# Attention and a two-layer MLP in one kernel: half of ten MLP blocks begun among the first heads, with fewer load buffers and w_in loaded by row halves

## The chip, the cores and the metric

The kernel runs on one core of one Trainium2 chip. The metric is the device time of one execution in microseconds (us). The kernel before took 426.06 us (median of 5 runs, 422.62 to 428.41).

## What is computed

`q`, `k` and `v` are fp32 arrays of 8 batches x 12 heads x 448 positions x 64. `w_in` is 768 x 2048 and `w_out` is 2048 x 768, both fp32. The output is 3584 x 768 fp32.

```python
scores = (1 / sqrt(64)) * q @ k.T                 # per batch and head, 448 x 448
attn = softmax(scores)
attn_out = attn @ v                               # 8, 12, 448, 64
x = attn_out.transpose(0, 2, 1, 3).reshape(8 * 448, 768)
h = x @ w_in
g = maximum(0.01 * h, h)
out = g @ w_out
```

## The kernel before

**Units.** Two heads make a unit `u`; there are 6 units a batch (`HP`) and 48 in all. A unit goes through these steps, each a function of the kernel:

- `load(u)` (L90): three DMAs of 224 KB, q, k and v in fp32, issued by SP in the order of the code (only the k of unit 0 is issued by ACT). The tiles come from a pool with 5 buffers for each of the three names.
- `cast(u)` (L103): POOL turns q, k and v into bf16 (L108, L109, L110). The q and k halves go into one tile of a pool of 4, v into one of 5 fixed tiles.
- `transposes(u)` (L163): eight PE transposes into PSUM (L169) and one DVE copy (L172) into `qkT`, for units 0 to 11; later units are turned by a DMA transpose that SP issues (L157).
- `scores(u, c)` (L176): two PE matmuls (L181) for each of 4 chunks of keys; `expo(u, c)` (L188): one ACT exponential (L190) over both heads.
- `pv(u, j)` (L192): sixteen PE matmuls (L199) for head `j`; a column of ones in v gives the softmax sums. DVE takes the reciprocals (L206) and multiplies (L207) into an x tile.
- `x_transposes(u)` (L211): four PE transposes (L220) and a DVE copy (L221) into `xT`, where the rows of the MLP's contraction are: unit `hp` of a batch is contraction slice `kk = hp`. From unit 9 on a DMA transpose does it.

**PSUM.** `scores` has 3 double-bank tiles of its own. Everything else on PE, the transposes, `pv`, and both products of the MLP, shares the two tiles with the tag "g" (`ps_g`), so that PE can write the third of these only when the first has been emptied.

**MLP.** The 3584 tokens are cut into 8 tiles of 384 and 512 tokens in turn (`cuts`); tile 0 has 384. `mlp(i)` (L242) makes for each of 16 blocks `m` six matmuls over `kk` (L250) and one Prelu on ACT from PSUM (L254), then for each 128 tokens and each half of the output 16 matmuls (L268), a DVE copy (L272) and the stores.

**Order.** Tile's scheduling is off, so each engine executes in the order in which the code issues. First the 6 units of batch 0 go through `first(u)` (L278), then the last two `pv` and transposes (L335 to L340). From there the MLP is a generator that yields after each block, and `cluster(g)` (L303), which holds 3 chunks of scores with the `pv`, casts, loads and transposes that belong to them, is called between yields when the matmul columns used have passed the next equal share (L352). Tile 0 has clusters 8 to 18, the first of them ahead of its first block. The third exponential of a cluster is put off to the next `settle()`, which follows the Prelu of a block.

**Weights.** `load_w()` (L119) issues the next weight DMA on POOL's software queue, in POOL's own order among the casts. It reads fp32 and writes bf16, 768 KB each. `w_in` comes in four steps of 512 columns with all 6 slices `kk`, `w_out` in four of 8 row blocks x 384 columns. One is issued ahead of `first(0)`; the others in `first(2)` (1), `first(3)` (2), `first(4)` (2) and `first(5)` (2), always ahead of that unit's cast.

Of the kernel before, what the change touches and what calls it, by code (L numbers as in the profile page):

```python
# [9 lines left out]
F32 = mybir.dt.float32  # L10
# [6 lines left out]
def kernel(  # L17
# [26 lines left out]

    const_pool = ctx.enter_context(tc.tile_pool(name="const", bufs=1))
    w_pool = ctx.enter_context(tc.tile_pool(name="weights", bufs=1))
    ld_pool = ctx.enter_context(tc.tile_pool(name="ld", bufs=5))
    cast_pool = ctx.enter_context(tc.tile_pool(name="cast", bufs=4))
    v_pool = ctx.enter_context(tc.tile_pool(name="vones", bufs=1))
    qk_pool = ctx.enter_context(tc.tile_pool(name="qk", bufs=1))  # L50
    exp_pool = ctx.enter_context(tc.tile_pool(name="exp", bufs=1))
    r_pool = ctx.enter_context(tc.tile_pool(name="rec", bufs=4))
    x_pool = ctx.enter_context(tc.tile_pool(name="x", bufs=3))
    xT_pool = ctx.enter_context(tc.tile_pool(name="xT", bufs=1))
    h_pool = ctx.enter_context(tc.tile_pool(name="h", bufs=2))
    o_pool = ctx.enter_context(tc.tile_pool(name="o", bufs=3))

# [53 lines left out]

    w_steps = []
    for i in range(4):
        w_steps.append((w_in_sb[:, :, ts(i, DF // 4)], w_in_v[:, :, ts(i, DF // 4)]))
    for i in range(4):
        at = (slice(None), ts(i % 2, MD // 2), ts(i // 2, NW))
        w_steps.append((w_out_sb[at], w_out_v[at]))
# [1 line left out]
    def load_w(n=1):  # L119
        for _ in range(n):  # L120
            if w_steps:
                o, i = w_steps.pop(0)
                nc.gpsimd.dma_start(out=o, in_=i)

    load(0, (nc.sync, nc.scalar, nc.sync))
    for i in range(1, 5):
        load(i)

    warm = const_pool.tile([P, 512], BF16)
# [15 lines left out]
        nc.gpsimd.memset(t[:, QL:], 0.0)  # L145
    cast(0, (nc.vector.tensor_copy, nc.scalar.copy, nc.gpsimd.tensor_copy))
    load_w()
    cast(1)
    cast(2)


    x_t = {}
# [35 lines left out]
    def expo(u, c):  # L188
        e = e_sb[u % NE][:, :EL].rearrange("p (j c s) -> p j c s", j=2, c=NSC)
        nc.scalar.activation(e[:, :, c, :], sc_t.pop((u, c))[:SC, :, :S], AX.Exp, scale=scale)  # L190
# [47 lines left out]
    def settle():  # L238
        while late:
            expo(*late.pop(0))  # L240

    def mlp(i):  # L242

        n = cuts[i + 1] - cuts[i]
        at = cuts[i] % NX
        h = h_pool.tile([P, MD, 4 * P], BF16, name="h")
        for m in range(MD):
            ps = ps_g.tile([P, 4 * P], F32, name="mm", tag="g")
            for kk in range(KD):
                nc.tensor.matmul(  # L250
                    ps[:, :n], w_in_sb[:, kk, ts(m, P)], xT[:, kk, at:at + n],
                    start=(kk == 0), stop=(kk == KD - 1),
                )
            nc.scalar.activation(h[:, m, :n], ps[:, :n], AX.Prelu, alpha=0.01)  # L254
            settle()
            yield KD * n

        todo = [(c, w) for c in range(n // P) for w in range(2)]
        if i == 0:
            todo.sort(key=lambda cw: cw[1])  # L260
        o = {}
        for c, w in todo:
            settle()
            if c not in o:
                o[c] = o_pool.tile([P, DM], F32, name="o")
            ps = ps_g.tile([P, 4 * P], F32, name="mm", tag="g")
            for m in range(MD):
                nc.tensor.matmul(  # L268
                    ps[:, :NW], h[:, m, ts(c, P)], w_out_sb[:, m, ts(w, NW)],
                    start=(m == 0), stop=(m == MD - 1),  # L270
                )
            nc.vector.tensor_copy(o[c][:, ts(w, NW)], ps[:, :NW])  # L272
            if w == 1:
                store(o.pop(c), cuts[i] + c * P)
            yield MD * NW


    def first(u):  # L278

        scores(u, 0)  # L280
        scores(u, 1)
        expo(u, 0)
        if u == 0:
            warm_up(4)
        expo(u, 1)
        if u >= 2:
            x_transposes(u - 2)
        if u >= 1:
            pv(u - 1, 0)
        load(u + 5)  # L290
        load_w({2: 1, 3: 2, 4: 2, 5: 2}.get(u, 0))
        if u + 1 < HP:
            transposes(u + 1)
        scores(u, 2)
        scores(u, 3)
        expo(u, 2)
        expo(u, 3)
        cast(u + 3)
        if u >= 1:
            pv(u - 1, 1)  # L300


    def cluster(g):  # L303
# [13 lines left out]
        for a, c in chunks[:2]:  # L317
            expo(a, c)
        late.extend(chunks[2:])
        for a, j in heads:  # L320
            pv(a, j)
            if j == 1 and a >= NPE - 3:
                x_transposes(a)
# [8 lines left out]
    warm_up(2)  # L332
    for u in range(HP):
        first(u)
    u = HP - 1  # L335
    pv(u, 0)
    x_transposes(u - 1)
    pv(u, 1)
    transposes(HP)
    x_transposes(u)  # L340


    begin = [8 * (i + 1) + 3 for i in range(B)]
    begin[0] = 8
    for i in range(B):
        work = list(range(begin[i], begin[i + 1])) if i + 1 < B else []
        n = cuts[i + 1] - cuts[i]
        total = MD * KD * n + n // P * MD * DM
        used, done = 0, 0
        lead = 1 if i == 0 else 0  # L350

        def catch_up():  # L352
            nonlocal done
            while done < len(work) and used * (len(work) - lead) >= total * (done + 1 - lead):
                settle()
                cluster(work[done])
                done += 1

        catch_up()
        for step in mlp(i):  # L360
            used += step
            catch_up()
# [30 lines left out]
```

The softmax here doesn't subtract the row's maximum and nothing guards it: scores larger than these inputs give would overflow.

## Time and profile before

The profiled execution took 426.06 us, of which 424.3 us are the span in which engines work; it is also the median one. The span by stage, from the trace (busy us of each engine in the stage; PE clock as a share of full speed):

| stage, us from the start | what runs | PE | DVE | ACT | POOL | PE clock | DMA, GB/s |
|---|---|---|---|---|---|---|---|
| 5 to 20 | units 0 to 3 | 12.05 | 6.13 | 11.92 | 8.20 | 1.00 | 250 |
| 20 to 36 | units 3 to 5, cluster 8 | 14.00 | 7.55 | 9.87 | 13.38 | 0.74 | 247 |
| 36 to 64 | MLP tile 0, first product, with clusters | 26.59 | 7.22 | 20.25 | 9.22 | 0.96 | 248 |
| 64 to 88 | MLP tile 0, second product, with clusters | 23.55 | 7.79 | 11.35 | 6.31 | 1.00 | 225 |
| 88 to 400 | tiles 1 to 7 | 310.99 | 65.90 | 173.37 | 52.91 | 1.00 | 132 |

Busy time of PE counts matmuls that run at half clock or that overlap in its pipeline, so a busy PE is not a full one. Where a view lists who waited, "PE tr L169 <- POOL qkb L109" means that PE's transposes at line 169 stood still until POOL's cast at line 109 had finished. "DMA fk<-in_k_dram" is a load of k, "SPq" and "POOLq" are the queues of DMA instructions on SP and POOL, q1 is the hardware queue of SP and q0 the software queue of POOL, which carries the weights only.

### The profile page before, as it was taken

What the parts mean: (1) busy time and instruction counts of PE and PEld (TensorE: products, weight loads), DVE (VectorE), ACT (ScalarE), POOL (GpSimd) and SP (SyncE); (2) the same over time, 40 slices, a digit from 0 to 9 for tenths busy, and PEclk for the clock granted to TensorE, in tenths of its full rate; (3) what the DMA queues carried; (4) which work ended last, traced back from release to release, by engine and by line L of the source; (5) the groups of instructions that cost most, each with busy time, mean ns of one, the idle gap of its engine ahead of it and who ended that gap; (6) DMA issues with size and microseconds to landing.
All of it is one profiled execution on the core that took longest, in us unless ns stands there. A gap on an engine that the chain in (4) does not pass through costs nothing.

```text
span 424.3 us, 8986 instructions
## 1 busy us (share of the span) xinstructions
PE 409.9 (97%) x3717; PEld 236.1 (56%) x3731; DVE 99.8 (24%) x271; ACT 228.3 (54%) x322; POOL 91.2 (21%) x168
## 2 busy tenths in 40 slices
PE   7789999999999999999999999999999999999995
PEld 2555556554565656554465656654465666654562
DVE  1552322320122312221132212321032311320021
ACT  4875773667724584467644476456742577214200
POOL 4494330431311212131130213122120200000000
PEclk9987999999999999999999999999999999999999
DMA  8999999996485946777365785779275420230022
GB/s 207 252 246 246 249 250 217 221 243 136 97 168 151 211 111 170 193 157 181 87 158 142 199 153 124 194 142 225 65 172 149 119 56 13 60 86 2 0 76 74
DMA packets 98505, 63.66 MB, mean 150 GB/s; under 512 B 55456, under 2 KB 94880, under 8 KB 98464
## 3 DMA queue, kind: packets, MB, share of 16 engines
q1 hardware_dynamic: 90928, 56.56, 56.3%
q0 software_dynamic: 7296, 6.29, 9.2%
q8 instruction: 29, 0.48, 0.5%
q10 hardware_dynamic: 240, 0.23, 0.2%
q14 instruction: 12, 0.10, 0.1%
HBM read 45.61 MB, written 11.01 MB: 133 GB/s over the span
## 4 chain that ended last, share of the span: by engine, by line
PE 90%; DMA 5%; DVE 2%; SPq 1%; issue 1%; ACT 1%; POOL 0%; ACTq 0%
PE mm L250 34%; PE mm L268 33%; PE pv L199 12%; PE sc L181 9%; DMA fk<-in_k_dram 2%; DMA fq<-in_q_dram 1%; DMA fv<-in_v_dram 1%; PE tr L169 1%; DVE x L207 1%; SPq L157 1%; DVE o L272 1%; ACT e L190 0%; SPq L97 0%; DVE rec L206 0%; PE tr L220 0%
## 5 line engine op out<-in xcount | busy, mean ns | idle before, releaser
L190 ACT ACTIVATE e<-sc 112x896 bf16<-112x896 f32 x192 | 164.4, 917 | 105.9 <-PE sc L181 105.7
L250 PE MATMUL mm<-xT,w_in_sb 128*128 128x384 bf16 (+1 forms) x754 | 150.6, 354 | 1.4 <-DVE x L207 0.7
L268 PE MATMUL mm<-w_out_sb,h 128*128 128x384 bf16 x896 | 150.5, 326 | 0.6 <-DVE x L207 0.3
L268 PEld LDWEIGHTS <-h 128*128 128x128 bf16 x896 | 85.8, 98 | 55.4 <-DVE x L207 0.5
L250 PEld LDWEIGHTS <-w_in_sb 128*128 128x128 bf16 x768 | 73.4, 98 | 67.1 <-issue 1.4
L254 ACT ACTIVATE h<-mm 128x384 bf16<-128x384 f32 (+1 forms) x128 | 69.6, 544 | 61.4 <-PE mm L250 60.3
L110 POOL CAST v<-fv 112x512 bf16<-112x512 f32 x48 | 29.6, 616 | 212.5 <-PE pv L199 184.3
L199 PEld LDWEIGHTS <-e 112*128 112x128 bf16 x1536 | 57.6, 99 | 29.8 <-issue 18.5
L199 PE MATMUL pv<-v,e 112*128 112x65 bf16 x1536 | 66.9, 195 | 2.8 <-ACT e L190 1.4
L272 DVE COPY o<-mm 128x384 f32<-128x384 f32 x56 | 31.2, 557 | 133.7 <-PE mm L268 133.7
L206 DVE RECIPROCAL rec<-pv 112x4 f32<-112x4 f32 x96 | 17.5, 182 | 158.8 <-PE pv L199 158.8
L181 PE MATMUL sc<-qkT 64*128 64x448 bf16 x384 | 49.8, 358 | 0.8 <-DVE qkT L172 0.4
L207 DVE TENSOR_TENSOR x<-pv,rec 112x256 bf16<-112x256 f32 x96 | 40.7, 424 | 3.3
L108 POOL CAST qkb<-fq 112x512 bf16<-112x512 f32 x47 | 28.9, 615 | 22.9 <-DMA qkT<-qkb 11.7
L109 POOL CAST qkb<-fk 112x512 bf16<-112x512 f32 x47 | 28.9, 614 | 10.4 <-DMA fk<-in_k_dram 10.3
L181 PEld LDWEIGHTS <-qkT 64*128 64x128 bf16 x384 | 13.8, 94 | 19.9 <-issue 10.7
L169 PE MATMUL tr<-ident,qkb 112*128 112x112 bf16 x96 | 8.3, 234 | 2.3 <-POOL qkb L109 1.7
L172 DVE COPY qkT<-tr 128x896 bf16<-128x896 bf16 x12 | 7.4, 620 | 12.7 <-PE tr L169 12.5
L169 PEld LDWEIGHTS <-qkb 112*128 112x128 bf16 x96 | 6.1, 109 | 4.6 <-POOL qkb L109 2.2
L135 PE MATMUL mm<-warm 128*128 128x512 bf16 x15 | 5.2, 486 | 1.2 <-DVE warm L130 1.2
L221 DVE COPY xT<-tr 128x448 bf16<-128x448 bf16 x9 | 3.5, 389 | 7.5 <-PE tr L220 7.5
L220 PE MATMUL tr<-ident,x 112*128 112x112 bf16 x36 | 3.7, 231 | 0.2
(17 smaller groups left out, 15.1 us busy)
## 6 DMA issues: line engine op xcount, KB each, us to landing
fq<-in_q_dram SPq DMA_DIRECT2D x48, 224.0 KB, 3.7
fv<-in_v_dram SPq DMA_DIRECT2D x48, 224.0 KB, 4.5
fk<-in_k_dram SPq DMA_DIRECT2D x47, 224.0 KB, 4.0
w_in_sb<-in_moe_w_in_dram POOLq DMA_DIRECT2D x4, 768.0 KB, 15.6
w_out_sb<-in_moe_w_out_dram POOLq DMA_DIRECT2D x4, 768.0 KB, 35.3
out_dram<-o SPq DMA_DIRECT2D x8, 336.0 KB, 3.0
out_dram<-o SPq DMA_DIRECT2D x8, 288.0 KB, 2.7
out_dram<-o SPq DMA_DIRECT2D x8, 240.0 KB, 3.2
```

Of the source, the lines that this page charges most:

```text
L108: by[0](qk_sb[u][:, 0].rearrange("p so h d -> p h so d"), fq)
L109: by[1](qk_sb[u][:, 1].rearrange("p so h d -> p h so d"), fk)
L110: by[2](v_sb[u % NV][:, :, :, :D], fv)
L169: nc.tensor.transpose(tr[:, i, ts(so, SC)], qk_sb[u][:, i, so], ident[:SC, :SC])
L181: nc.tensor.matmul(ps[:, j, :S], t[j * D:(j + 1) * D, S + c * SC:S + c * SC + P], t[j * D:(j + 1) * D, :S], start=True, stop=True,)
L190: nc.scalar.activation(e[:, :, c, :], sc_t.pop((u, c))[:SC, :, :S], AX.Exp, scale=scale)
L199: nc.tensor.matmul(ps[:, qc, :], e[:, at:at + P], vt[:, j, c, :], start=(c == 0), stop=(c == NSC - 1),)
L207: nc.vector.tensor_mul(x_t[u][:, :, j, :], ps[:SC, :, :D], rec.to_broadcast([SC, NSC, D]))
L250: nc.tensor.matmul(ps[:, :n], w_in_sb[:, kk, ts(m, P)], xT[:, kk, at:at + n], start=(kk == 0), stop=(kk == KD - 1),)
L254: nc.scalar.activation(h[:, m, :n], ps[:, :n], AX.Prelu, alpha=0.01)
L268: nc.tensor.matmul(ps[:, :NW], h[:, m, ts(c, P)], w_out_sb[:, m, ts(w, NW)], start=(m == 0), stop=(m == MD - 1),)
L272: nc.vector.tensor_copy(o[c][:, ts(w, NW)], ps[:, :NW])
```

## The change

- The load pool goes from 5 to 3 buffers, the pool of cast q and k from 4 to 2. Three units are loaded ahead instead of five; units 3 and 4 are loaded between the first casts, and in `first(u)` the load of unit `u + 5` comes after the cast of unit `u + 3` instead of ahead of the transposes. `cast(2)` moves into `first(0)`.
- `w_in` is loaded by halves of the contraction (3 slices `kk`) and halves of the columns (1024), upper half first, still four DMAs of 768 KB. Two of them are issued ahead of `first(0)`, one each in `first(2)` and `first(3)`; `w_out` in `first(4)` and `first(5)` as before.
- `fill(1)` makes one block's sum over `kk` = 0, 1, 2 (three matmuls of 384 columns) in a "g" tile, and DVE copies it in fp32 to SBUF (`part`). Ten are made: three in `first(4)`, three in `first(5)`, two after it and two in cluster 8.
- In tile 0's first product these ten blocks then have three matmuls (`kk` = 3, 4, 5), a DVE add of the PSUM sum to `part`, and the Prelu reads `part` in SBUF. The other six blocks are whole and stand between them.
- `transposes(6)` moves into `first(5)`; `x_transposes(5)` moves into cluster 8, which is called ahead of the MLP; clusters 9 to 18 are spread over tile 0's remaining columns.

```diff
--- before.py
+++ after.py
@@ -44,14 +44,15 @@
 
     const_pool = ctx.enter_context(tc.tile_pool(name="const", bufs=1))
     w_pool = ctx.enter_context(tc.tile_pool(name="weights", bufs=1))
-    ld_pool = ctx.enter_context(tc.tile_pool(name="ld", bufs=5))
-    cast_pool = ctx.enter_context(tc.tile_pool(name="cast", bufs=4))
+    ld_pool = ctx.enter_context(tc.tile_pool(name="ld", bufs=3))
+    cast_pool = ctx.enter_context(tc.tile_pool(name="cast", bufs=2))
     v_pool = ctx.enter_context(tc.tile_pool(name="vones", bufs=1))
     qk_pool = ctx.enter_context(tc.tile_pool(name="qk", bufs=1))
     exp_pool = ctx.enter_context(tc.tile_pool(name="exp", bufs=1))
     r_pool = ctx.enter_context(tc.tile_pool(name="rec", bufs=4))
     x_pool = ctx.enter_context(tc.tile_pool(name="x", bufs=3))
     xT_pool = ctx.enter_context(tc.tile_pool(name="xT", bufs=1))
+    part_pool = ctx.enter_context(tc.tile_pool(name="part", bufs=1))
     h_pool = ctx.enter_context(tc.tile_pool(name="h", bufs=2))
     o_pool = ctx.enter_context(tc.tile_pool(name="o", bufs=3))
 
@@ -111,7 +112,8 @@
 
     w_steps = []
     for i in range(4):
-        w_steps.append((w_in_sb[:, :, ts(i, DF // 4)], w_in_v[:, :, ts(i, DF // 4)]))
+        at = (slice(None), ts(i // 2, KD // 2), ts(i % 2, DF // 2))
+        w_steps.append((w_in_sb[at], w_in_v[at]))
     for i in range(4):
         at = (slice(None), ts(i % 2, MD // 2), ts(i // 2, NW))
         w_steps.append((w_out_sb[at], w_out_v[at]))
@@ -123,7 +125,7 @@
                 nc.gpsimd.dma_start(out=o, in_=i)
 
     load(0, (nc.sync, nc.scalar, nc.sync))
-    for i in range(1, 5):
+    for i in range(1, 3):
         load(i)
 
     warm = const_pool.tile([P, 512], BF16)
@@ -145,8 +147,10 @@
         nc.gpsimd.memset(t[:, QL:], 0.0)
     cast(0, (nc.vector.tensor_copy, nc.scalar.copy, nc.gpsimd.tensor_copy))
     load_w()
+    load(3)
     cast(1)
-    cast(2)
+    load_w()
+    load(4)
 
 
     x_t = {}
@@ -239,21 +243,55 @@
         while late:
             expo(*late.pop(0))
 
+
+
+    NF = 10
+    part = part_pool.tile([P, NF, cuts[1]], F32)
+    begun = []
+
+    def fill(m_count):
+        for _ in range(m_count):
+            m = len(begun)
+            if m == NF:
+                return
+            begun.append(m)
+            ps = ps_g.tile([P, 4 * P], F32, name="mm", tag="g")
+            for kk in range(KD // 2):
+                nc.tensor.matmul(
+                    ps[:, :cuts[1]], w_in_sb[:, kk, ts(m, P)], xT[:, kk, :cuts[1]],
+                    start=(kk == 0), stop=(kk == KD // 2 - 1),
+                )
+            nc.vector.tensor_copy(part[:, m], ps[:, :cuts[1]])
+
     def mlp(i):
 
         n = cuts[i + 1] - cuts[i]
         at = cuts[i] % NX
         h = h_pool.tile([P, MD, 4 * P], BF16, name="h")
-        for m in range(MD):
+        order = range(MD)
+        if i == 0:
+
+            whole = list(range(NF, MD))
+            order = [0, 1]
+            for m in range(2, NF):
+                order += whole[:1] + [m]
+                whole = whole[1:]
+            order += whole
+        for m in order:
             ps = ps_g.tile([P, 4 * P], F32, name="mm", tag="g")
-            for kk in range(KD):
+            k0 = KD // 2 if i == 0 and m < NF else 0
+            for kk in range(k0, KD):
                 nc.tensor.matmul(
                     ps[:, :n], w_in_sb[:, kk, ts(m, P)], xT[:, kk, at:at + n],
-                    start=(kk == 0), stop=(kk == KD - 1),
+                    start=(kk == k0), stop=(kk == KD - 1),
                 )
-            nc.scalar.activation(h[:, m, :n], ps[:, :n], AX.Prelu, alpha=0.01)
+            g = ps[:, :n]
+            if k0:
+                g = part[:, m]
+                nc.vector.tensor_add(g, g, ps[:, :n])
+            nc.scalar.activation(h[:, m, :n], g, AX.Prelu, alpha=0.01)
             settle()
-            yield KD * n
+            yield (KD - k0) * n
 
         todo = [(c, w) for c in range(n // P) for w in range(2)]
         if i == 0:
@@ -277,6 +315,7 @@
 
     def first(u):
 
+        f = 1 if u >= 4 else 0
         scores(u, 0)
         scores(u, 1)
         expo(u, 0)
@@ -287,17 +326,21 @@
             x_transposes(u - 2)
         if u >= 1:
             pv(u - 1, 0)
-        load(u + 5)
-        load_w({2: 1, 3: 2, 4: 2, 5: 2}.get(u, 0))
-        if u + 1 < HP:
-            transposes(u + 1)
+        load_w({2: 1, 3: 1, 4: 2, 5: 2}.get(u, 0))
+        fill(f)
+        transposes(u + 1)
+        fill(f)
         scores(u, 2)
         scores(u, 3)
         expo(u, 2)
         expo(u, 3)
+        if u == 0:
+            cast(2)
         cast(u + 3)
+        load(u + 5)
         if u >= 1:
             pv(u - 1, 1)
+        fill(f)
 
 
     def cluster(g):
@@ -317,6 +360,10 @@
         for a, c in chunks[:2]:
             expo(a, c)
         late.extend(chunks[2:])
+        if g == 2 * 4:
+            fill(1)
+            x_transposes(HP - 1)
+            fill(1)
         for a, j in heads:
             pv(a, j)
             if j == 1 and a >= NPE - 3:
@@ -332,31 +379,31 @@
     warm_up(2)
     for u in range(HP):
         first(u)
-    u = HP - 1
-    pv(u, 0)
-    x_transposes(u - 1)
-    pv(u, 1)
-    transposes(HP)
-    x_transposes(u)
+    fill(1)
+    x_transposes(HP - 2)
+    fill(1)
+    pv(HP - 1, 0)
+    pv(HP - 1, 1)
+    cluster(8)
 
 
     begin = [8 * (i + 1) + 3 for i in range(B)]
-    begin[0] = 8
+    begin[0] = 9
     for i in range(B):
         work = list(range(begin[i], begin[i + 1])) if i + 1 < B else []
         n = cuts[i + 1] - cuts[i]
         total = MD * KD * n + n // P * MD * DM
+        if i == 0:
+            total -= NF * KD // 2 * n
         used, done = 0, 0
-        lead = 1 if i == 0 else 0
 
         def catch_up():
             nonlocal done
-            while done < len(work) and used * (len(work) - lead) >= total * (done + 1 - lead):
+            while done < len(work) and used * len(work) >= total * (done + 1):
                 settle()
                 cluster(work[done])
                 done += 1
 
-        catch_up()
         for step in mlp(i):
             used += step
             catch_up()
```

## The prediction

> **What bounds the kernel now.** I read the engine totals first. PE is busy in 409.9 of 424.3 us, so only idle or half-speed PE time can be won. The table of stages says where that is: after 64 us PE hardly pauses, before it the clock falls. Then the same table in steps of a microsecond, of which these are the lines around 20 and 33 us (columns: busy us of PE, PEld, DVE, ACT, POOL, then PE clock, DMA share, GB/s):
>
> ```profile
> 19.00:20.00 1.00, 0.12 (x3) 0.12 (x4) 0.00 (x0) 0.00 (x0) 0.61 (x1) 1.00 1.14 317
> ...
> 22.00:23.00 1.00, 1.00 (x14) 0.68 (x11) 0.29 (x2) 1.00 (x2) 1.00 (x3) 0.50 1.11 250
> ...
> 33.00:34.00 1.00, 0.83 (x7) 0.45 (x8) 0.92 (x2) 0.00 (x0) 0.83 (x2) 0.50 1.17 243
> ```
>
> PE stood at 19 us and ran at half clock at 22 and at 33 us, while DMA moves about 245 GB/s throughout. The chain of waits tells why PE stood:
>
> ```profile
> 8.59 10.57 DMA fk<-in_k_dram
> ...
> 19.21 0.62 POOL qkb L109
> ...
> 19.88 0.37 PE tr L169 x4
> ...
> 35.92 5.01 PE mm L250 x24
> ```
>
> The k of unit 4 was 10.57 us on its way, POOL cast it, and only then came unit 4's transposes. The fourth line is where tile 0 begins: at 35.92, at half clock at first, since 24 matmuls take 3.90 us later (the chain at 141.97 us). The stage up to 20 us is thus held by transfers. The DMA queues in the windows 22 to 24 us and then 28 to 30 us (packets, MB, share of time):
>
> ```profile
> q1 hardware_dynamic: 528, 0.51, 112.4%
> ```
>
> ```profile
> q0 software_dynamic: 238, 0.24, 71.8%
> q1 hardware_dynamic: 237, 0.23, 43.0%
> ```
>
> While a weight step is moved, loads fall from 528 to 237 packets per 2 us: it takes half of the DMA.
>
> [...]
>
> **Part 1: thirty matmuls moved, none removed.** Tile 0's first product has 96 matmuls of 384 columns; 30 go to the earlier stage. At 0.1625 us each (3.90 / 24) that is 4.9 us taken out of the time after tile 0's start, call it S (35.9 before). If PE is dense before S, the half clock in its first 24 matmuls goes too: 5.01 - 3.90 = 1.1 us. Sum: 6.0 us. The time is then unchanged if S moves 6.0 us later, less what part 3 costs.
>
> **Part 2: where S goes.** Two steps of w_in (unit rows 0 to 2) now come before the loads of units 3 to 5 instead of one. Check of the method on before: k of unit 4 is the 14th load; 14 x 0.229 MB + one weight step of 0.786 MB = 4.0 MB, at 245 GB/s 16.3 us, from a start at about 2.6 us 18.9; the chain has 19.16. Now: unit 5's k is the 17th load. 17 x 0.229 + 2 x 0.786 = 5.47 MB, 22.3 us, so 24.9 us; weight packets of twice the size are in no row: [...] I take 25.7. With the cast (0.62 us) unit 5's transposes end their wait at 26.4, where they ran at 23.6 before. POOL's issue of the second w_in step (0.82 to 0.95 us) stands ahead of cast(2), which can wait, since its data come at 9.5.
>
> From there to S the "g" tiles see twenty users in turn: transposes of units 5, 6 and 7 (DVE copy 0.62 us each), five pv (reciprocal and multiply 0.60), three x transposes (0.39), and nine of the ten fills (I count all ten). DVE: 1.9 + 3.0 + 1.2 + 10 x 0.557 = 11.6 us. PE: 24 transposes at 0.07, 18 score matmuls at 0.112, five pv at 0.62, three x transposes at 0.3, ten fills at 0.49: 12.6 us at full clock. With two tiles a user costs half of PE time + DVE time + two handovers of about 0.05 us, (0.55 + 0.6 + 0.1) / 2 = 0.63 to 0.7 us; twenty are 12.6 to 14.2 us. I take 13.6, and 1.0 for a half clock after the wait for loads [...]. S = 26.4 + 13.6 + 1.0 = 41.0.
>
> A floor under S: transposes(7) stand ahead of S and the third block (a whole one, `m` = 10) needs the last quarter of w_in. 23 loads and four weight steps are 8.42 MB, 34.4 us of DMA, so 37.0, with cast, transposes and landing about 38. Before it was 23 loads and two steps, 6.85 MB, 30.5 us: covered by S at 35.9. This is the step that eats the gain.
>
> **Part 3: the ten halves in tile 0.** Ten DVE adds (5.6 us of an engine that is busy 7.2 of 28 us there) are hidden in sum; their Prelus read SBUF: nearest rows are ACT's cast from SBUF, 619 ns for 512 columns, against a Prelu from PSUM of 512, 597, so +0.02 us each, 0.2 us of ACT in all. But half blocks take PE 0.49 us, and a whole block's tile is freed only by ACT. On ACT behind a cluster stand two exponentials (1.72 us), the Prelu of a half that waits for its add (0.17 + 0.56 + handovers after its matmuls), the third exponential (0.83) and only then the whole block's Prelu. PE is then two blocks further and wants that tile: I count 0.9, 1.0, 0.3 and 0.2 us for the four intervals between clusters 8 and 12, 2.4 us; before there is one such wait of 0.4 (pv after the Prelu L254). Net 2.0; bounds 0.5 (ACT catches up) and 4 (1 us in each).
>
> **Part 4: fewer buffers.** From tile 1 on a load has two to three clusters (about 6 us each) to land, against 3.7 to 4.5 us from issue to landing, and a cast's tile is freed by the DMA transpose of two units before, issued two clusters earlier. I put the cost at 0 because those clusters hide it; if one load or transpose stood in the path, the waits of SP queued behind it (loads, xT transposes, stores) would hold PE each time. The moved load issues (0.31 to 0.46 us of SP each) stay in order, and SP waits on the landings anyway. The later w_out steps wait behind the cast of unit 6 on POOL, to about 37 us; two are moved at half share (6.4 us each) from about 41 and land at 54; they are needed at S + 18 = 59 (66 matmuls, 10.7 us, with three clusters and the waits of part 3).
>
> **Sum.** S later by 5.1 us; taken out 6.0; added 2.0: +1.1 us on 424.3, and 1.8 us lie around the span (426.06 - 424.3). The profiled execution equals the median, so 427.1; I say 427.0. About 1% (4.3 us) is what a measurement of this kernel can tell from no change.
>
> **Rivals.**
> - *The second half of w_in comes late* (slower). Its steps are issued on POOL behind the casts of units 4 and 5, at about 25 and 28.5 us; before, a step's first packets came 4 to 5 us after its issue and it took 6.4 us at half share. Then they land at 36.4 and 42.8, and block `m` = 10 is wanted at S + 1.3 = 42.3. Each microsecond later stands PE for one; it decides from 45.5 on, with what part 3 costs. For it: the DMA is full. Against: three load buffers hold loads back, and twice the packet size gives the weights more than half. With S at 43.5 (ends of part 2's bounds) and 1.5 us of wait: 431.
> - *Shallow buffers pace the later tiles* (slower). One late landing of 0.5 us in each of some 30 units: 440. Against: part 4. For: no row of before shows what three and two buffers do.
> - *The fills fit into idle PE time for nothing* (faster). PE idles or waits for 2 to 3 us before 36 and is halved for 10 of them. If S is at the floor, 38, and part 3 costs 1: 424.3 + 2.1 - 6.0 + 1.0 = 421.4 span, 423; all at its best, 421.5. More than that the DMA floor forbids.
> - That the ten fills aren't early at all can't be: they only need units 0 to 2 and two weight steps that landed near 20 us.
>
> **How the numbers follow.** The forecast (no change) 0.48, late w_in 0.34, paced tiles 0.08, fitting fills 0.10. Slower by over 1%: three quarters of the second, all of the third, 0.04 of the first, 0.37. Faster by over 1%: 0.06 of the last and 0.02 of the first, 0.08. Same 0.55. The forecast's own range is 424 to 430; with late w_in's larger part and the fitting fills 422.5 to 433.5.
>
> **What would show it.** Right: unit 5's transposes end their wait near 26; tile 0's block `m` = 0 starts near 41; PE clock 1.00 from there; waits of PE's L250-type matmuls on Prelus in the first product of about 2 us; nothing new after 88 us. Wrong: S under 39 or over 43; a PE wait on w_in's DMA at the third block; load or cast waits in the later tiles; or a half clock running through units 3 to 5[...].

## The result and the profile after

The kernel after took 429.65 us (median of 27 runs, 426.64 to 431.66), the kernel before 425.16 us (median of 48 runs on the same chips, 421.89 to 428.67). The ratio is 1.0109, 95% interval 1.0091 to 1.0126: slower by 4.5 us. The predicted 427.0 is 2.65 us too low. The measured time lies inside the range of 422.5 to 433.5, but no change was forecast, and the loss is clear of the interval. The profiled execution's span is 429.7 us, 5.4 us over that of before; it is one of the slowest executions of after (431.50 us).

The chain of waits of the kernel after has the two places where the time went:

```profile
8.66 12.41 DMA fk<-in_k_dram
...
21.13 0.62 POOL qkb L110
...
21.80 0.56 PE tr L173 x4
...
41.87 0.66 PE mm L284 x3
...
88.33 6.05 DMA xT<-x
94.43 1.67 PE mm L284 x7
```

Against before: the k of unit 4 is 12.41 us on its way instead of 10.57, and unit 4's transposes run at 21.80 instead of 19.88. Tile 0 begins at 41.87 instead of 35.92, 6.0 us later. And the chain now goes through a transfer in the second tile, which it did not before: the DMA transpose of the attention output (`xT<-x`), issued at 88.33, landed at 94.38. PE's waits in the whole of the kernel after have only two of over 2 us after the start-up; the first is at unit 4, the second that transfer (us in total, times, longest):

```profile
PE tr L173 <- POOL qkb L110: 2.9, 2, 2.6
PE mm L284 <- DMA xT<-x: 2.1, 1, 2.1
```

The table in steps of a microsecond, in the columns that the prediction named:

```profile
20.00:21.00 1.00, 0.00 (x0) 0.00 (x0) 0.00 (x0) 0.00 (x0) 0.00 (x0) 1.00 1.07 226
...
22.00:23.00 1.00, 1.00 (x8) 0.24 (x6) 0.61 (x1) 0.05 (x1) 0.00 (x0) 0.50 1.11 356
...
36.00:37.00 1.00, 0.55 (x7) 0.31 (x5) 0.85 (x2) 0.00 (x0) 0.00 (x0) 1.00 1.12 231
```

At 20 to 21 us every engine stands and only DMA works: the pause before unit 4 has become longer, and none of the ten fills is in it. At 22 us the clock is halved, from 21.0 to 27.9. At 36 us the clock is full, but PE works only 0.55 of the microsecond, while DVE is busy 0.85 of it: these are the fills. In before, this was a stage at half clock (0.50 at 33 us and on to 38).

A cut of the time that all kernels below share: S is the start of tile 0's first matmul and T1 that of tile 1's, both from the trace in order of time. From T1 on the kernels take 336.4 us (one variant 336.9), plus what they wait at tile 1 on the xT transpose and, in two runs, what a half clock after that wait costs. (The chain has S of before at 35.92; in order of time its first matmul starts at 35.71.)

| | S | S to T1 | T1 | wait on xT | span |
|---|---|---|---|---|---|
| before, the profile shown | 35.71 | 52.2 | 87.91 | 0 | 424.3 |
| after | 41.87 | 49.17 | 91.04 | 2.14 | 429.7 |
| difference | +6.2 | -3.0 | +3.1 | +2.1 | +5.4 |

### The profile page after: what moved, and what is told of

Same layout as the page of the kernel before. It is cut to its first block, busy times and chain, and to the rows that moved or that the text cites. A ratio compares the mean times of both kernels' runs of the same rounds, so it can differ in the third digit from the quotient of the medians.

```text
span 429.7 us, 9081 instructions
## 1 busy us (share of the span) xinstructions
PE 410.0 (95%) x3717; PEld 234.3 (55%) x3731; DVE 110.1 (26%) x291; ACT 228.8 (53%) x322; POOL 90.7 (21%) x168
## 4 chain that ended last, share of the span: by engine, by line
PE 87%; DMA 6%; DVE 3%; ACT 1%; SPq 1%; issue 1%; POOL 1%
PE mm L306 33%; PE mm L284 31%; PE pv L203 12%; PE sc L185 9%; DMA fk<-in_k_dram 3%; DMA xT<-x 1%; DMA fv<-in_v_dram 1%; PE mm L260 1%; DMA fq<-in_q_dram 1%; DVE x L211 1%; PE tr L173 1%; DVE part L264 1%; DVE o L310 1%; ACT h L292 1%; DVE part L291 1%
## 5 line engine op out<-in xcount | busy, mean ns | idle before, releaser
L284 PE MATMUL mm<-xT,w_in_sb 128*128 128x512 bf16 (+1 forms) x724 | 145.5, 353 | 4.5 <-DMA xT<-x 2.1
L284 PEld LDWEIGHTS <-w_in_sb 128*128 128x128 bf16 x738 | 70.1, 98 | 68.7 <-issue 5.0
L292 ACT ACTIVATE h<-mm 128x512 bf16<-128x512 f32 (+1 forms) x118 | 64.7, 548 | 59.6 <-PE mm L284 58.4
L310 DVE COPY o<-mm 128x384 f32<-128x384 f32 x56 | 31.2, 558 | 134.0 <-PE mm L306 134.0
L260 PE MATMUL mm<-xT,w_in_sb 128*128 128x384 bf16 x30 | 7.0, 345 | 1.1 <-DVE part L264 0.9
L292 ACT ACTIVATE h<-part 128x384 bf16<-128x384 f32 x10 | 5.2, 522 | 3.5 <-DVE part L291 3.1
L291 DVE TENSOR_TENSOR part<-part,mm 128x384 f32<-128x384 f32 x10 | 5.5, 553 | 6.0 <-PE mm L284 6.0
```

The costliest lines, as they stand in the source:

```text
L284: nc.tensor.matmul(ps[:, :n], w_in_sb[:, kk, ts(m, P)], xT[:, kk, at:at + n], start=(kk == k0), stop=(kk == KD - 1),)
L292: nc.scalar.activation(h[:, m, :n], g, AX.Prelu, alpha=0.01)
```

## The experiments

Three questions: which part of the change moves S, what the fills cost where they stand, and whether they would be free elsewhere. My theory after the result had three parts: a second weight step ahead of the loads moves S by about 6 us, the half blocks give back only 3 us of tile 0, and the shallow buffers make PE wait at tile 1; to the fills it gave 3 to 4 us. The first part was the prediction's own account, that the loads hold S back. The first rival was that the fills themselves are the loss: PE is not idle where they stand. The second was that the later wait at tile 1 makes the difference and the fills are harmless.

### The parts alone

**Buffers alone** (before, with the after's pools and places of the loads):

```
-ld_pool bufs=5, cast_pool bufs=4
+ld_pool bufs=3, cast_pool bufs=2
-    for i in range(1, 5): load(i)      # then cast(0) load_w() cast(1) cast(2)
+    for i in range(1, 3): load(i)      # then cast(0) load_w() load(3) cast(1) load(4)
+    load(u + 5) after cast(u + 3) in first(u); cast(2) in first(0)
```

> The kernel before with the changed kernel's 3 load and 2 cast buffers and its places of the loads and casts, and nothing else of the change. Theory (three parts: tile 0 starts about 6 us later because a second w_in step goes ahead of the loads of units 3 to 5, the halves give back only 3 us of tile 0, and shallow buffers make PE wait 2.1 us on an xT DMA transpose at tile 1): tile 0 starts within 1 us of 35.7, and the wait on the xT transpose is there, so +1 to +3 us. Rival (the shallow buffers are most of the loss): +4 to +5.5 us. Rival (the wait at tile 1 belongs to the shifted order of tile 0's clusters, not to the buffers): within 1 us of before, no wait on xT.

Measured: ratio 1.0104 (1.0068 to 1.0140), 428.68 us. S is 35.06 and T1 86.30, both earlier than in the profile of before. The loss stands at tile 1, and the waits of this run from 68 us on, first PE's and then SP's, name it:

```profile
PE mm L251 <- DMA xT<-x: 2.7, 1, 2.7
```

```profile
SPq L97 <- POOL qkb L108: 3.0, 1, 3.0
```

The second line is the load of unit 16 at 74.79: with three buffers it needs the tile that POOL's cast of unit 13 empties, and that cast was late (74.15). In before the same load went out at 73.42, without that wait. Behind it SP issues transposes, stores and loads without a gap up to the xT transpose of unit 11 at 84.75, which lands 5.42 us later; PE needed it at about 87.4 and got it at 90.2. Before issued it at 84.37, 3.5 us ahead of T1 (here 1.6), and it landed after 3.4 us. The clock was 0.50 from 89.9 to 93.4, 1.6 us more. So the loss is the 4 to 5.5 us of the rival, not the 1 to 3 of the theory. All four executions of this kernel lie between 426.4 and 427.2 us of span, 3.7 us or more above the 422.7 that this run's T1 gives without the wait; that fits a loss of this size in all of them, though only one has a profile. In the profile of after no load waits for its tile between 68 and 92 us, so this row of causes is shown for the buffers alone.

**Weights alone** (before, with `w_in` by row halves and two steps ahead of `first(0)`):

```
-        w_steps.append((w_in_sb[:, :, ts(i, DF // 4)], w_in_v[:, :, ts(i, DF // 4)]))
+        at = (slice(None), ts(i // 2, KD // 2), ts(i % 2, DF // 2))
+        w_steps.append((w_in_sb[at], w_in_v[at]))
...
+    load_w()                            # behind cast(1)
-        load_w({2: 1, 3: 2, 4: 2, 5: 2}.get(u, 0))
+        load_w({2: 1, 3: 1, 4: 2, 5: 2}.get(u, 0))
```

> The kernel before with w_in in row halves, two steps ahead of first(0), one each in first(2) and first(3); buffers as before, no fills. Theory: unit 4's transposes wait until about 21.8 instead of 19.9 us, [...]tile 0 starts near 38 to 39 us, and its third or fifth block may wait for the last w_in step: +2 to +4 us. Rival (total DMA decides, the order of the weights doesn't): tile 0 starts within 1 us of 35.7 and the time within 1 us of before.

> The run with the weights alone once more: its profiled execution was the shortest of six by 1.5 us, with a clock of 0.989 against 0.981 to 0.988. If it loses in half-clock windows that come and go, this profile shows one or two more of them than the first one, ahead of or in tile 0; if the loss is a wait for the last w_in step, PE waits in tile 0's first blocks.

Measured: 1.0103 (1.0055 to 1.0150), 429.19 us. The first profile was the shortest of its six executions (424.9 us of span; the others 426.4 to 430.1) and has S at 37.47; a second profile of the same kernel has S at 39.72 and a span of 428.1. In both, unit 4's transposes wait twice, for the q and then for the k, about 4.25 us in all, and the first half clock lasts 6.8 us (3.4 us in before, 21.0 to 24.4). The second has another half clock, from 34.8 to 41.7 us, around the start of tile 0. So the new cut of the weights and the second step ahead of the loads move S by 1.8 us in the shortest execution against the profile of before (2.7 against its second profile, below), and by more where the clock falls again.

**No fills** (after with `NF = 0`: all sixteen blocks whole, everything else as in after):

> The changed kernel with no fills and all sixteen blocks whole; buffers, loads and weights as changed. Theory: the fills delay tile 0's start by about 3 to 4 us (30 matmuls and ten copies between tiles that share two PSUM buffers) and give back 3, so tile 0 starts near 37.5 and the time is within 1.5 us of the changed kernel. Rival (the fills are a true gain that the loads hide): 3 to 5 us slower than the changed kernel. Rival (the fills are the loss): 3 to 5 us faster than the changed kernel, as fast as before.

Measured: 1.0064 (1.0029 to 1.0100), 427.49 us. Its chain:

```profile
8.64 13.33 DMA fk<-in_k_dram
...
36.07 4.06 PE mm L284 x24
...
84.92 6.22 DMA xT<-x
```

This run decides for the first rival, where S is concerned. The loads come as late as in after (13.33 against 12.41 us), the same two weight steps stand ahead of them, and tile 0 still begins at 36.07. The fills alone move S by 41.87 - 36.07 = 5.8 us, where the theory had 3 to 4; in three other profiles with all ten fills in these places (two of them below with one other thing changed) S is 41.1 to 42.0. The wait on xT is here too (2.8 us and 1.7 us of half clock), and the twelve spans fall into two groups, 422.1 to 425.1 and 426.3 to 428.1, which suggests that it comes and goes. Without both, this execution would have 423.5 us of span, 4.0 less than after's 427.5 without the wait (below): the fills cost 5.8 us ahead of S and bring back 1.9 behind it. The medians differ by less, about 1.9 us (the rival had 3 to 5), because the kernel without fills shows the upper group in half of its executions.

This kernel also has the changed order of work (`transposes(6)`, `x_transposes(5)` and cluster 8), which was not run alone; its S lies ahead of the 37.47 of the weights alone.

**Before, a second profile**, to see how S varies without any change:

> The kernel before once more, unaltered, for a second profile: other executions of it were 1 to 2 us shorter than the profiled one. If the half-clock windows ahead of 38 us make the difference, tile 1 starts near 86 with a clock above 0.99, and from there to the end it is 336.4 us again. If not, the difference lies after tile 1's start.

Measured: span 422.2 us, S at 34.76, T1 at 85.80, clock 1.00 at 33 and 35 us; tile 0's first 24 matmuls take 3.90 us by its chain, where the prediction's line has 5.01:

```profile
34.92 3.90 PE mm L250 x24
```

The second half-clock stretch of before, from 32 to 38 us, isn't there in every execution.

### What the fills cost where they stand

**After again**, and **load 17 moved** (in cluster 16 to 17, the load of unit 17 goes behind the xT transpose of unit 11):

```
+            if g == 17: load(17)
+            if g != 16:
-            load(u + 5 + r)
+                load(u + 5 + r)
```

> The changed kernel once more, unaltered, for a second profile. From the profiles so far the span is the start of tile 1 plus 336.4 us plus the wait on the xT transpose there (and 1.7 us more where a half clock follows it). Theory (the wait comes and goes between executions): either the wait of about 2 us is there again and the span is near 429.5, or it is absent and the span is near 427.5; tile 0 starts at 41 to 42 us and tile 1 at 90.5 to 91.5 in both cases. Rival (the wait is fixed): it is there with 2 us and the span near 429.5.

> The changed kernel, but the load of unit 17 is issued in cluster 17, after the DMA transpose of unit 11's x, instead of in cluster 16 just ahead of it. Theory (that transpose landed after 6.0 us instead of 3.4 since three loads were queued ahead of it): PE's wait on xT at tile 1 goes, 1.5 to 2.1 us faster than the changed kernel. Rival (the transpose is slow for another reason, such as the stores or transposes next to it): the wait stays, no gain.

Measured: after again 1.0099 (1.0060 to 1.0139), with a profile of 427.5 us, S 41.98, no wait on xT. With the load moved 1.0116 (1.0069 to 1.0163), profile 426.6 us, no wait either. The second rival falls with the first of these: an execution of after without the wait is still 5.3 us longer than the second profile of before. The wait that the first profile of after shows isn't typical: three executions of after have 429.7 us of span or more, and the median is 427.9. Whether the moved load takes the wait out can't be read from one profile without it, since after again has none either; the median didn't fall, within an interval of about 2 us either way.

**Full clock** (after, with 14 matmuls on zeros ahead of unit 4's transposes):

> The changed kernel with 14 matmuls on zeros (3.0 us of PE at full clock, results unused) ahead of the transposes of unit 4, where PE waits for k. Theory (the two half-clock windows from 21 to 27.6 us come from that pause and lie on the path): the clock stays 1.00, tile 0 starts 1 to 2 us earlier (near 40), 1 to 2 us faster. Rival (units 4 and 5 are paced by the two shared PSUM tiles and DVE, the clock is hidden): the clock stays 1.00 but tile 0 starts within 0.5 us of 41.9, no gain.

Measured: 1.0071 (1.0048 to 1.0094). The clock is 1.00 from 16 to 45 us, S is 40.95. Half clock in the kernel after is thus worth 0.9 us of S, between what theory and rival expected. It is no share of the 5.8 us, since the run without fills has the same half clock, from 20.7 to 27.5 us.

**No copies** (the fills' matmuls are made, their sums neither copied nor added), and a variant in which only the copies were left out and `part` was zeroed at the start:

```
-            nc.vector.tensor_copy(part[:, m], ps[:, :cuts[1]])
...
-                g = part[:, m]
-                nc.vector.tensor_add(g, g, ps[:, :n])
+                g = ps[:, :n]
```

> The changed kernel with neither the ten copies nor the ten adds: the begun sums are dropped and the ten half blocks' Prelus read their second-half sum from PSUM, so that half of the contraction is missing from ten blocks. Theory (DVE's copies pace the fills through the two PSUM tiles): tile 0 starts at 39 to 40.2 with a similar half clock; the stretch to tile 1 stays within 1 us of 49.2, since ACT's order is the loss there. Rival (PE's work alone moves the start): 41 to 42. Rival (DVE's adds are tile 0's loss): the stretch falls below 47.7.

> The changed kernel without the ten DVE copies of the begun blocks: their matmuls run at the same places but their sums are dropped, and part holds zeros set at the start, so that the first half of the contraction is missing from ten blocks. Theory (between unit 5's transposes and tile 0 the fills are paced by the handover of the two shared PSUM tiles through DVE, not by PE's work): tile 0 starts at 38.5 to 40 instead of 41.9. Rival (thirty matmuls of 4.9 us simply stand on PE's path): tile 0 starts at 41 to 42.

Measured: 1.0040 (1.0021 to 1.0059), S 39.26, with a half clock as long as after's, 1 us earlier. The last fill runs into unit 7's transposes and these into tile 0, with no wait between them:

```profile
38.24 0.65 PE L260 MATMUL mm<-xT,w_in_sb 128*128 128x384 bf16 x3
38.86 0.55 PE L173 MATMUL tr<-ident,qkb 112*128 112x112 bf16 x8
39.26 0.65 PE L283 MATMUL mm<-xT,w_in_sb 128*128 128x384 bf16 x3
```

The variant also gave 1.0040 (1.0015 to 1.0064), but its memset held DVE at the start and shifted the units (PE waited 2.9 us on DVE there), so its S of 39.5 isn't compared. From the first: 41.87 - 39.26 = 2.6 us of the 5.8 are the copies, the other 3.2 the matmuls. Thirty matmuls are 4.9 us of PE, so some 1.7 us of them did fit into time in which PE stood; the copies took more than that back. The timeline of after around two fills shows how a copy costs PE time although neither engine is full (from 28 us to S PE is busy 12.0 of 13.9 us, DVE 9.9):

```profile
36.07 0.56 DVE L264 COPY part<-mm 128x384 f32<-128x384 f32 x1 [0.29 <-PE mm L260]
...
36.69 0.65 PE L260 MATMUL mm<-xT,w_in_sb 128*128 128x384 bf16 x3 [0.45 <-DVE part L264]
...
37.37 0.56 DVE L264 COPY part<-mm 128x384 f32<-128x384 f32 x1 [0.44 <-PE mm L260]
```

DVE starts when PE's three matmuls end, PE's next fill starts when DVE's copy ends: 0.45 us of standing on one side, 0.44 on the other. The two shared tiles are handed back and forth. Ten fills for 5.8 us are 0.58 us each: half of the sum of a fill on PE (0.49) and its copy on DVE (0.56), and the handovers.

**Exponentials later** (after, but `settle()` only behind whole blocks):

```
-            settle()
+            if not k0: settle()
```

> The changed kernel, but in tile 0 the third exponential of a cluster is settled only after a whole block's Prelu (or ahead of the next cluster), not after a half block's. Theory (a whole block's PSUM tile waits on ACT behind the half's Prelu and that exponential; tile 0 took 3.0 us more than its work asks): the stretch from tile 0's start to tile 1's start falls from 49.2 to 47.7 to 48.5 us. Rival (the loss is in DVE's adds and their handover, not in ACT's order): within 0.3 us of 49.2.

Measured: 1.0059 (1.0030 to 1.0087); S to T1 48.24 instead of 49.17, 0.9 us less. This is the wait on ACT, in the timeline of after:

```profile
48.78 0.52 ACT L292 ACTIVATE h<-part 128x384 bf16<-128x384 f32 x1 [0.19 <-DVE part L291]
...
49.21 0.90 ACT L194 ACTIVATE e<-sc 112x896 bf16<-112x896 f32 x1
...
50.00 0.48 ACT L292 ACTIVATE h<-mm 128x384 bf16<-128x384 f32 x1
...
50.54 0.67 PE L203 MATMUL pv<-v,e 112*128 112x65 bf16 x16 [0.58 <-ACT h L292]
```

The Prelu of a half block is followed by the put-off exponential, and only then comes the Prelu of a whole block, whose PSUM tile PE's `pv` wants: 0.58 us of standing.

### Elsewhere

**In the pause** (after with eight blocks begun over `kk` = 0, 1, all of them ahead of unit 4's transposes, copied by DVE and ACT in turn; first in after's order of blocks and with the exponentials put off to whole blocks, then in the natural order, with the exponentials after each block and load 17 moved):

```
-    NF = 10
+    NF = 8; KF = 2
-        fill(f) in first(4) and first(5)
+        if u == 3: fill(NF)
+                if m % 2: nc.scalar.copy(part[:, m], ps[:, :cuts[1]])
...
-            order = [0, 1]; for m in range(2, NF): ...      # the second only
+            order = list(range(MD))
```

> The changed kernel with the begun blocks put where PE really pauses: eight blocks over kk = 0 and 1 only, all in first(3) ahead of unit 4's transposes, their sums copied by DVE and ACT in turn (ACT pauses there as well); the third exponential settled after whole blocks only. Theory (a begun block costs nothing only inside a pause, and a half block in tile 0 loses about half of what it saves): no wait for k at 19 to 22, clock 1.00, tile 0 starts at 35 to 36.5, the stretch to tile 1 is 49 to 50, tile 1 near 85.5, so 3 to 5 us faster than the changed kernel and within 2 us of before. Rival (begun blocks delay whatever they stand in, since the shared PSUM tiles pass them on): tile 0 starts at 38 or later, no faster than the changed kernel with no fills.

> As the run with eight blocks begun over kk = 0 and 1 in the pause of first(3), but tile 0's blocks in their natural order (the last w_in step is first needed at block 8), the exponential settled after each block, and unit 17's load after the xT transpose of unit 11. Theory (a begun block is free only in a real pause): tile 0 starts at 35 to 36, no wait for w_in, the stretch is 49 to 50.3, tile 1 starts near 85 to 86, the span is 421.5 to 422.5, 1 to 2 us faster than the median of before. Rival (what a begun block saves is lost again at its DVE add and Prelu): the stretch is 51 or more, as fast as before or slower.

Measured: the first gave 1.0100 (1.0065 to 1.0135), with S at 35.33. What ate it stands in its chain, after the row of fills in front of unit 4:

```profile
27.42 13.38 DMA w_in_sb<-in_moe_w_in_dram
40.80 0.05 issue
40.85 1.31 PE mm L288 x7
```

The third block of tile 0 needs the last quarter of `w_in`, and that landed at 40.8: PE stood 3.1 us, and a half clock from 42.0 on followed (still 0.50 from 44 to 45 us). With the natural order, where the blocks of that quarter come last, the ratio is 0.9970 (0.9953 to 0.9987), 423.76 us. In its timeline the fills fill the pause:

```profile
18.45 0.49 PE L261 MATMUL mm<-xT,w_in_sb 128*128 128x384 bf16 x2
19.31 3.65 PE L261 MATMUL mm<-xT,w_in_sb 128*128 128x384 bf16 x14 [0.38 <-DVE x L211]
```

They end at 22.96, no wait on unit 4's cast is left, the clock is 1.00 from 16 to 45 us, S is 35.17 and S to T1 49.28. (This profile is the shortest of its 20 executions, 420.8 us of span; the median is 422.0.)

**Before, warmed** (matmuls on zeros in its two pauses, 8 ahead of unit 4's transposes and 6 behind `first(5)`; then the same with load 17 moved):

> The kernel before with 8 matmuls on zeros ahead of unit 4's transposes and 6 ahead of the last unit's pv (results unused), which fill PE's two pauses. Theory (the half clock at 21 to 24 and 32 to 38 us costs about 1 and 1.5 us): clock 1.00 up to tile 0, which starts 1 to 2 us earlier at full clock; 1 to 3 us faster than before. Rival (before 36 us the exponentials and loads set the pace): within 1 us of before.

> The kernel before with the matmuls on zeros in PE's two pauses and unit 17's load behind the xT transpose of unit 11. With the matmuls alone the executions fell into two groups of spans, near 421.3 and near 424.3, at the same clock. Theory (the upper group has the wait on that transpose): only the lower group is left, the median is 1 to 1.5 us faster than before. Rival (the groups have another cause): both groups again, as fast as before.

Measured: 1.0000 (0.9977 to 1.0023), no gain, with two groups of spans, 420.9 to 422.5 and 423.3 to 424.6; with the load moved as well 0.9958 (0.9942 to 0.9975), 423.58 us, all 22 spans between 421.0 and 423.4. S is 34.21 and 33.65, the clock 1.00 from 16 to 45 us in both. This is the lowest ratio of the study, though its interval overlaps that of the run before it: without a single fill, and with pauses filled with useless matmuls, the kernel is as fast as the version that puts useful ones there. The span's upper group went with the load's move, but for 423.2 to 423.4 in three executions, which speaks for before having the wait on xT in a part of its executions; no profile of before caught it.

## Why the prediction was off, point by point

**The sum.** Predicted +1.1 us on the profile of before, measured +5.4 between the two profiles. S came 1.1 us later than counted (+6.2 instead of +5.1; 0.2 of it is only where S of before is read), tile 0 gave back 1.0 us less (3.0 instead of 4.0), and the wait at tile 1 came on top (2.1, counted as 0): 1.1 + 1.1 + 1.0 + 2.1 = 5.3.

That wait isn't typical of after, so the +4.5 us of the medians has to be explained without it. The sum put the span of after at 424.3 + 1.1 = 425.4 us; after again, without the wait, has 427.5. Of these 2.1 us, 1.0 is S (41.98 for 41.0) and 1.0 is part 3. Another 0.9 us is the profile of before, which was taken for the median: that was true of the five runs shown, and the median of 48 is 0.9 us lower. With 0.4 us between after again and the median of after (427.9 of span), 1.1 + 2.1 + 0.9 + 0.4 = 4.5. The terms that failed are thus the start of part 2's stretch (26.4 us, measured 27.3), part 3 (2.0, measured 3.0) and the one profile of before, taken for the usual one.

Part 1 has a share in the 0.9. The half clock at the start of tile 0 that it took out, 1.1 of its 6.0 us, is in one profile of before and not in the other: against an execution without it, the thirty matmuls are a gain of 4.9 us, and tile 0 gives back 1.9, not 3.0 (51.04 to 49.17).

**Part 2, S = 41.0: nearly the right number, and a floor that was not there.** The twenty users of two tiles held in size: from unit 5's transposes to S the sum has 14.6 us, the trace 27.3 to 41.87, and the handovers of 0.45 and 0.44 us are what the model describes. The start was 0.9 late (27.3 for 26.4). What failed is the floor of 38 us, of which I wrote "This is the step that eats the gain": the run without fills has S at 36.07 with the same loads. The floor counted all four weight steps ahead of unit 7's k and had it at 37.0; in after this k landed at 30.38, with the third weight step only under way, and the last step landed at 40.31. So transfers were not what moved S to 41.87. It is the fills, 5.8 us for 4.9 us of matmuls. With a floor at 38 they seemed to cost 3 us of S; ten users at my own 0.63 to 0.7 us are 6.3 to 7. Had I asked what S is with the loads late and no fills, I would have seen that the same matmuls are charged again ahead of S, for more than they give back in tile 0.

**Where PE waits.** Predicted: unit 5's transposes end their wait at 26.4. In the trace the wait is at unit 4 (2.6 us, until 21.80); unit 5's transposes follow without one at 27.3. The step between is half clock from 21.0 to 27.9, for which I counted 1.0, an estimate of mine; the warmed run prices it at 0.9. A half clock running through units 3 to 5 was one of the signs of being wrong, and it is what stood there. The queue model was right on the load itself: unit 5's k landed at 25.41, estimated between 24.9 and 25.7, but PE wasn't yet waiting for it. The trace also shows how the two sizes of packets share DMA, in the window 12 to 14 us of after:

```profile
q0 software_dynamic: 156, 0.32, 83.9%
q1 hardware_dynamic: 159, 0.15, 29.1%
```

The two queues still move nearly equal numbers of packets, 156 and 159 here, as 238 and 237 in before. With row halves a weight packet is twice as large (0.32 MB in 156 packets, where before has 0.24 in 238), so the weights get two thirds of the 0.47 MB, and loads fall to 159 packets, where they have 237 beside a weight step in the prediction's lines of before. I take this for the reason why the k of unit 4 came 1.9 us later; the 25.7 had 0.8 us for two such steps (24.9 without), an estimate of mine that no row of before supports. No run has the larger packets without the second step ahead of the loads. But in before the one step was only just through when this k landed, 775 packets by 19.16 us, so a second one behind it with packets of the old size would hardly have touched it.

**Part 3, the half blocks: 3.0 us instead of 2.0.** The mechanism named, ACT's order before a whole block's Prelu, is there, but it is 0.9 us of the 3.0 by the run that changes the order. The adds cost next to nothing, as predicted (S to T1 48.99 without them, 49.17 with). DVE's row of the page has the add at 553 ns, close to before's copy of 384 from PSUM (L272, 557 ns), as I had estimated, and the Prelu from SBUF takes 522 ns:

```profile
L292 ACT ACTIVATE h<-part 128x384 bf16<-128x384 f32 x10 | 5.2, 522 | 3.5 <-DVE part L291 3.1
L291 DVE TENSOR_TENSOR part<-part,mm 128x384 f32<-128x384 f32 x10 | 5.5, 553 | 6.0 <-PE mm L284 6.0
```

The other 2 us hardly show as waits. After the change of order the listed waits in tile 0's first product sum up to 1.3 us, against 1.1 in the run without fills. But a matmul is recorded as 0.32 us long while the next starts 0.1625 us after it, so a stand of PE of up to 0.16 us isn't listed at all. The first blocks of tile 0 show it, in after and then without fills:

```profile
41.87 2.92 PE L284 MATMUL mm<-xT,w_in_sb 128*128 128x384 bf16 x15 [0.25 <-DVE part L264]
```

```profile
36.07 4.06 PE L284 MATMUL mm<-xT,w_in_sb 128*128 128x384 bf16 x24
```

At the pace of the second line (24 x 0.1625 + 0.16 = 4.06) fifteen matmuls take 2.60 us; three half blocks and a whole one took 2.92. Counted from the start of a matmul to the start of the next, between S and T1, PE loses 3.2 us behind `w_in` matmuls in after, 2.3 after the change of order, and under 0.1 in the run without fills. So the other 2 us stand at the borders of blocks too. That it is the handover of the two tiles, as ahead of S, is likely and not shown by a run of its own.

**Part 4, fewer buffers: 0 was wrong.** "If one load or transpose stood in the path, the waits of SP queued behind it would hold PE each time" was the mechanism, and I set it at nothing because clusters hide it. In the run with buffers alone one load did stand in the path: it waited 3.0 us for its tile, and PE 2.7 us at the end of that row. In after itself the term is 2.1 us in one profile and nothing in the other. It isn't paced in each unit, as the rival had it, but happens once, where tile 1 needs the last head pair of its batch and SP's queue is densest.

**The rivals.** *Late w_in* did not occur in after, since S was late enough; it is real (landing 40.8, estimated 42.8), shown where S was made early. *Fitting fills* named the right idle time in the wrong place. In the run without fills PE's waits from 28 us to S sum up to 0.7 us, so there was little to fit into; the time that stands free is the pause at 18 to 22 us. Even there the fills won little: against the warmed before with the same load moved, S is 1.5 us later (35.17 to 33.65) and tile 0 gives back 1.75 (49.28 to 51.03). The two kernels differ in buffers and weight steps as well, so the 1.5 us are not the fills' alone.

**What stays open.** Buffers alone and weights alone each cost about 4.4 us, both together with the new order and without fills only 2.7 (1.0064); the parts don't add, and the new order wasn't run alone. Half-clock stretches and the wait on xT come and go between executions, and I could not say in advance in which. That the median of after didn't fall with the load moved fits a wait that after has seldom.

## What to carry to other kernels

Work moved forward costs least where its engine really stands (here ten fills outside the pause moved S by 5.8 us, and with eight in it S was 35.17, as early as in before): find the microseconds in which the row of that engine is empty, and put it exactly there; ask of the model what the later mark would be without the moved work. In a stage in which PE and DVE pass two PSUM tiles to and fro, an extra user costs more than its PE time: here 0.58 us for 0.49, half of what it takes of both engines and the handovers. And a shallower pool must be checked at the one point where the queue behind it is densest, not by its average slack.

## What was not expected of the hardware

- A wait of PE of 2.7 us (buffers alone) or 2.8 us (no fills) at tile 1 went with a half clock of 3.4 us (from 89.9 and from 92.4), 1.6 to 1.7 us lost; one of 2.1 us (after) did not. In before a wait of 1.7 us, until 19.88, was followed by a half clock at 21.0, which lasted 3.4 us; the second one of before, from 31.2 to 38.0, lasted 6.8 us and is there in one execution and not in the other. The length of a listed wait thus didn't tell whether a half clock would follow.
- The first weight step on the software queue moved its first packets 5 to 6 us after its issue (before: issued at 6.21, none by 12.0, six by 12.5; after: issued at 6.45, four by 12.0). The prediction had 4 to 5; later steps took 4.9 (before, issued at 21.43) and 3.8 (after, issued at 24.55).
- The same DMA transpose took 3.4 us from issue to landing in before and 5.4, 6.0 and 6.2 us in the three profiles with three load buffers that show the wait, each time behind the three DMAs of one load and two stores on the same queue. What makes the difference is open: in before these five started 3.4 us ahead of it instead of 2.8, but in after again 2.9, and there it landed after 3.8.
